# Dropping two doubly computed blocks of group 0, and regrouping the idle products of the opening

## The chip, the cores and the metric

The kernel runs on one core of a Trainium2 chip. The metric is the device time of one execution in microseconds. The core has a matrix engine (TensorE, PE in the profile, whose weight loads are listed apart as PEld), a vector engine (VectorE, DVE), a scalar engine (ScalarE, ACT), a general engine (GpSimd, POOL) and a synchronisation engine (SyncE, SP). Each runs its own instructions in order and waits for the others by semaphores. PSUM holds the results of TensorE in eight banks. Transfers between memory and the core are issued by POOL (the inputs) and SP (transposing loads and stores).

## What is computed

The reference is linear attention with a decay per head, followed by a two-layer perceptron with an exact GELU. Batch 4, heads 8, sequence 768, head size 64; the perceptron goes 512 to 2048 to 512.

```python
# attention, for each batch and head, blocks of 64 positions
intra = einsum('bhic,bhjc->bhij', qb, kb) * Dmask         # lam**(i-j) for i >= j
intra = einsum('bhij,bhjd->bhid', intra, vb)
inter = einsum('bhid,bhde->bhie', qb * lam_pow, kv_state)  # lam**(i+1)
out[:, :, sl] = intra + inter
kv_state = lam**64 * kv_state + einsum('bhsd,bhse->bhde', kb * rev_pow, vb)
# perceptron over all 4*768 = 3072 tokens
h = x @ w_in
g = 0.5 * h * (1 + erf(h / sqrt(2)))
result = g @ w_out
```

## The kernel before

The tokens are cut into chunks of 128 positions of one batch. A group is the same chunk position of all four batches: T = 512 tokens, and there are NG = 6 groups. Attention fills the activations `x_t` of a group (128 x 4 x 512, bf16), one quarter of the columns per batch (`empty`, line 337, a multiplication on VectorE). The perceptron `mlp(g)` (line 412) then works on the group.

The first product of a group has 16 blocks `kf` of 128 hidden units. A block is four TensorE products of 128x128 weights by 512 columns (`columns`, line 419), accumulated in one PSUM bank, then one GELU on ScalarE into `g_t` (line 430). The second product has 16 pieces p0 to p15 (line 455): four products each, with the weights `w_out_t`.

`mlp` returns a list of named blocks, and `run_blocks` (line 501) issues them in that order. A dictionary, written out by hand, gives the work to be issued ahead of a named block: loads, copies, and the attention of the next group (`visit`). Issue order is execution order on each engine.

With `n2 > 0`, a few blocks are split by columns, so that they can begin when only half of `x_t` is filled: a0 and a1 do columns 0 to 255 of blocks 0 and 1, and b0 and b1 the rest, with the GELU of all 512 columns behind each b. Group 0 is called as `mlp(0, 2)`, so n2 = 2 and n3 = 0. Line 482 then lists blocks m0 to m15 whole, from `n3`. Blocks 0 and 1 are in that list as well: they are computed by a0, a1, b0, b1 and again by m0 and m1, which write the same values to the same place. Their PSUM bank is chosen by line 427: blocks 0 and 1 use the banks `mo0` and `mo1` in both computations, the others alternate between two banks `mh`. Group 1 is called with n2 = 4 and n3 = 6, later groups with neither; in these no block is listed twice.

The opening, ahead of group 0's perceptron, is the attention of the first four chunks, which has no earlier state: transposes, `scores0`, masks, and `outputs0` (line 379), eight small products for each chunk which read the values `v_t` (one tile for chunks 0 and 1, one for 2 and 3). Into this the kernel puts idle products (`keep_warm`, line 494): 128x512 products of a zeroed tile into a bank that nobody reads. It issues one ahead of the four `outputs0`, and two behind each of them.

The inputs arrive in the order of the list on line 147, all issued by POOL: keys and queries of the first chunks, values `v_t`, then the first weights in five steps, `i0-2` (hidden blocks 0 and 1), `i2-4`, `i4-8`, `i8-12`, `i12-16`, each as two transfers; then the second weights in four steps `o0-4` to `o12-16`, mixed with the inputs of group 1. The semaphores of these transfers go round in eight, so transfer number i + 8 is issued only when number i has landed.

Of the kernel before, what the change touches and what calls it, by code (L numbers as in the profile page):

```python
# [15 lines left out]
def kernel(  # L16
# [19 lines left out]
    NK2 = d_ff // 128  # L36
    T = B * C
# [16 lines left out]
    def bank(shape, dtype, tag, name):  # L54
        return ps.tile(shape, dtype, tag=tag, name=name, bufs=BANKS[tag])
# [280 lines left out]
    def empty(c):  # L336
        nc.vector.tensor_mul(xT[c.g][:, :, c.b * C:(c.b + 1) * C], c.o, lam_o)  # L337
# [41 lines left out]
    def outputs0(n):  # L379
        c = live[n]  # L380
        c.o = bank([128, HP, C], F32, "at", "o_ps")
        issue([[(c.o[half(1 - hi), hp, :], c.v[:, 2 * hp + hi, :], c.sm[:, hp, hi, :], True) for hi in range(2)]
               for hp in range(HP)])
# [28 lines left out]
    def mlp(g, n2=0, n3=0):  # L412


        x_t = xT[g]
        g_t = g_pool.tile([128, NK2, T], BF16, tag="g", name="g_t")
        hs = {}

        def columns(kf, lo, up):
            for ki in range(NK1):  # L420
                nc.tensor.matmul(hs[kf][:, lo:up], w_in_t[:, ki, kf * 128:(kf + 1) * 128], x_t[:, ki, lo:up],  # L421
                                 start=(ki == 0 and lo == 0), stop=(ki == NK1 - 1), skip_group_check=True)

        def mm1(kf, lo, up, last):
            def run():
                if lo == 0:
                    hs[kf] = bank([128, T], F32, f"mo{kf}" if kf < min(n2, 2) else "mh", "h_ps")
                columns(kf, lo, up)
                if last:
                    nc.scalar.activation(g_t[:, kf, :up], hs[kf][:, :up], ACT.Gelu)  # L430
            return run

        def rest(kfs):
            def run():
                h_ps = bank([128, len(kfs), C], F32, "mh", "h_ps")
                for i, kf in enumerate(kfs):
                    for ki in range(NK1):
                        nc.tensor.matmul(h_ps[:, i, :], w_in_t[:, ki, kf * 128:(kf + 1) * 128], x_t[:, ki, T - C:],  # L438
                                         start=(i == 0 and ki == 0), stop=(ki == NK1 - 1), skip_group_check=True)
                nc.scalar.activation(g_t[:, kfs[0]:kfs[-1] + 1, T - C:], h_ps, ACT.Gelu)  # L440
            return run

        om = {}

        def store(io, ps_, w):
            n = w.stop - w.start
            o_sb = out_pool.tile([128, n], F32, tag=f"o_{n}", name="o_sb")
            r = io * S + g * C
            nc.scalar.copy(o_sb, ps_)  # L449
            if g == 0:  # L450
                held.append((r, w, o_sb))
            else:
                nc.sync.dma_start(out[r:r + C, w], o_sb)

        def mm2(io, part):
            def run():
                if part == 0:
                    om[io] = bank([128, d_model], F32, "mh" if g == 0 and io >= 2 else f"mo{io % 2}", "o2_ps")
                for kf in range(part * 4, part * 4 + 4):
                    nc.tensor.matmul(om[io], g_t[:, kf, io * C:(io + 1) * C], w_out_t[:, kf, :],  # L460
                                     start=(kf == 0), stop=(kf == NK2 - 1))
                if part == NK2 // 4 - 1:
                    store(io, om[io], slice(0, d_model))
            return run

        def mm2_half(io, h):
            def run():
                w = slice(h * (d_model // 2), (h + 1) * (d_model // 2))
                o2 = bank([128, d_model // 2], F32, f"mo{(io + h) % 2}", "o2_ps")
                for kf in range(NK2):  # L470
                    nc.tensor.matmul(o2, g_t[:, kf, io * C:(io + 1) * C], w_out_t[:, kf, w],  # L471
                                     start=(kf == 0), stop=(kf == NK2 - 1))
                store(io, o2, w)
            return run

        blocks = [(f"a{kf}", mm1(kf, 0, 2 * C, False)) for kf in range(n2)]

        blocks += [(f"b{kf}", mm1(kf, 2 * C, T - C if kf < n3 else T, True))
                   for kf in [*range(2, n2), *range(min(n2, 2))]]
        blocks += [(f"m{kf}", mm1(kf, 0, T - C, True)) for kf in range(n2, n3)]  # L480
        blocks += [(f"l{i}", rest(list(range(i, min(i + 4, n3))))) for i in range(0, n3, 4)]
        blocks += [(f"m{kf}", mm1(kf, 0, T, True)) for kf in range(n3, NK2)]
        if g == 0:
            second = [mm2(io, part) for part in range(4) for io in range(B)]
        elif g == NG - 1:
            second = [mm2(io, part) for io in range(B - 1) for part in range(4)]
            second += [mm2_half(B - 1, h) for h in range(2)]
        else:
            second = [mm2(io, part) for io in range(B) for part in range(4)]
        return blocks + [(f"p{i}", run) for i, run in enumerate(second)]  # L490
# [3 lines left out]
    def keep_warm(n):  # L494
        if not idle_ps:
            idle_ps[0] = bank([128, 512], F32, "mo0", "idle_ps")
        for _ in range(n):
            nc.tensor.matmul(idle_ps[0], idle[:, :128], idle, start=True, stop=True)  # L498
# [34 lines left out]
    scores0(3)  # L533
    make_lam()
    nc.scalar.activation(warm, pos, ACT.Gelu)
    keep_warm(1)
    for n in range(B):
        outputs0(n)
        empty(live[n])
        keep_warm(2)  # L540


    alloc_x(1)
# [11 lines left out]
    def ahead_of_group_1():  # L555
# [10 lines left out]
        begin(9)  # L566

    run_blocks(mlp(0, 2), {
        "m2": [ahead_of_group_1],
        "m6": [make_dmask] + [lambda n=n: decay_k0(n, nc.vector) for n in range(B)],  # L570
# [70 lines left out]
    for g in range(1, NG):  # L641
        if g + 1 < NG:
            alloc_x(g + 1)
        run_blocks(mlp(g, 4, 6) if g == 1 else mlp(g), plan_of(g))
# [29 lines left out]
```

## Time and profile before

| | us |
|---|---|
| median of the runs | 212.78 |
| the profiled execution, its own time | 212.92 |
| span of the profile (first to last instruction) | 211.1 |
| PE busy | 200.6 |
| POOL busy | 102.6 |
| ACT busy | 91.1 |
| DVE busy | 82.8 |

The span is 1.8 us shorter than the execution's time; what lies around it is outside the program's instructions. The profile's columns for a stretch of time (a timeline) are: start in us from the first instruction, length in us, engine, line, operation, what it writes and reads, shape, count, and in brackets the engine's idle time before it with what ended it. A row can stand for many instructions, and its length runs from the start of the first to the end of the last. The single record of a matmul includes its way through the array (0.38 us for a 128x512 product), while in a stream such products begin 0.22 us apart: a count of products is therefore turned into time by the distance of starts and not by the mean of the records. A few matmul records are missing: 62 are listed where 64 were issued.

### The profile page before, as it was taken

Reading aid. Unit: us, or ns where it says so; the run is one execution under the profiler, and the core shown is the slowest. Engines: PE = TensorE matmul, PEld = TensorE weight load, DVE = VectorE, ACT = ScalarE, POOL = GpSimd, SP = SyncE. Lnnn points to the kernel's source line nnn. Section 1 sums busy time; section 2 is a strip of 40 time slices with the busy share of each in tenths; the row PEclk is TensorE's granted clock in tenths of the full one; section 3 lists DMA queues with packets and bytes.
Section 4 is the critical chain, followed back from the end, with each engine's and each line's share of the span. In section 5 each row is a group of like instructions: output and inputs, shape, how many; then the busy total and the mean of one; then the engine's idle time right before and its main releaser. Section 6 shows DMA issues by size and latency. Waiting matters only on the chain.

```text
span 211.1 us, 5565 instructions
## 1 busy us (share of the span) xinstructions
PE 200.6 (95%) x2393; PEld 101.9 (48%) x2423; DVE 82.8 (39%) x185; ACT 91.1 (43%) x166; POOL 102.6 (49%) x144
## 2 busy tenths in 40 slices
PE   7789999999999999999999999999999999999992
PEld 2545445546754444444444444544444444444461
DVE  3578604037935556717525725532330331000000
ACT  5484664247666312266311456221556211665120
POOL 8978545798999008999169999300000000000000
PEclk9999999999999999999999999999999999999999
DMA  6999999999999995999999999412100021100121
GB/s 59 148 171 205 205 189 176 187 119 147 122 179 176 201 137 72 116 154 225 150 132 109 233 188 147 80 53 99 51 3 0 3 99 53 50 0 0 53 91 60
DMA packets 94713, 24.49 MB, mean 116 GB/s; under 512 B 86880, under 2 KB 91744, under 8 KB 94688
## 3 DMA queue, kind: packets, MB, share of 16 engines
q0 software_dynamic: 73536, 13.64, 79.6%
q1 hardware_dynamic: 21152, 10.50, 25.0%
q8 instruction: 19, 0.31, 0.6%
q14 instruction: 6, 0.05, 0.1%
HBM read 27.27 MB, written 6.29 MB: 159 GB/s over the span
## 4 chain that ended last, share of the span: by engine, by line
PE 86%; POOL 3%; DMA 3%; DVE 2%; ACT 2%; issue 2%; POOLq 0%
PE h_ps L421 38%; PE o_ps L460 37%; DMA v_t<-in_v_dram 3%; PE sc_ps L345 3%; POOL kq_t L82 3%; PE o_ps L345 2%; PE kv_ps L345 2%; PE o_ps L471 2%; ACT g_t L430 1%; PE idle_ps L498 1%; PE t_ps L250 1%; DVE x_t L337 1%; DVE sm L291 1%; PE h_ps L438 1%; PE t_ps L246 0%
## 5 line engine op out<-in xcount | busy, mean ns | idle before, releaser
L421 PE MATMUL h_ps<-x_t,w_in_t 128*128 128x512 bf16 (+3 forms) x404 | 85.8, 363 | 1.3 <-ACT g_t L430 0.2
L460 PE MATMUL o_ps<-w_out_t,g_t 128*128 128x512 bf16 x353 | 80.3, 379 | 1.9 <-issue 1.7
L430 ACT ACTIVATE g_t<-h_ps 128x512 bf16<-128x512 f32 (+1 forms) x98 | 57.3, 591 | 33.4 <-PE h_ps L421 33.4
L421 PEld LDWEIGHTS <-w_in_t 128*128 128x128 bf16 x416 | 39.3, 98 | 43.0 <-issue 1.4
L460 PEld LDWEIGHTS <-g_t 128*128 128x128 bf16 x368 | 34.6, 98 | 40.1
L337 DVE TENSOR_TENSOR x_t<-o_ps,lam_o 128x512 bf16<-128x512 f32 x24 | 16.6, 691 | 65.0 <-PE o_ps L345 64.8
L449 ACT COPY o_sb<-o_ps 128x512 f32<-128x512 f32 (+1 forms) x25 | 14.2, 568 | 63.9 <-PE o_ps L460 61.3
L280 POOL TENSOR_TENSOR vd<-vg_t,lam_v 128x512 bf16<-128x512 bf16 x20 | 21.3, 1070 | 19.7 <-DMA vg_t<-in_v_dram 18.7
L291 DVE TENSOR_TENSOR sm<-sc_ps,dmask 128x512 bf16<-128x512 f32 x20 | 13.6, 682 | 13.5 <-PE sc_ps L345 13.5
L71 POOL DMA_DIRECT2D k_t<-in_k_dram x20 | 18.1, 905 | 1.6 <-DMA w_out_t<-in_moe_w_out_dram 1.4
L106 POOL DMA_DIRECT2D vg_t<-in_v_dram x20 | 16.5, 847 | 2.1 <-DMA w_in_t<-in_moe_w_in_dram 2.0
L267 POOL COPY k<-k_t 64x256 bf16<-64x256 bf16 x34 | 13.7, 404 | 2.2 <-DMA k_t<-in_k_dram 1.2
L71 POOL DMA_DIRECT2D q_t<-in_q_dram x16 | 14.4, 901 | 0.0
L271 DVE COPY k<-k_t 64x256 bf16<-64x256 bf16 x34 | 11.8, 348 | 0.5
L345 PEld LDWEIGHTS <-kqT 64*64 64x64 bf16 (+1 forms) x352 | 7.4, 107 | 9.4 <-issue 8.3
L498 PE MATMUL idle_ps<-idle 128*128 128x512 bf16 x28 | 9.5, 441 | 1.3 <-DVE idle L151 1.2
L345 PE MATMUL sc_ps<-kqT 64*64 64x64 bf16 (+1 forms) x352 | 10.4, 197 | 0.1
L345 PE MATMUL o_ps<-sm,vg_t 64*64 64x64 bf16 x320 | 8.4, 193 | 0.0
L345 PE MATMUL kv_ps<-vd,k 64*64 64x64 bf16 x288 | 8.0, 193 | 0.0
L316 DVE TENSOR_TENSOR state<-t,lam_c 128x256 bf16<-128x256 f32 x16 | 7.0, 438 | 0.5
L125 POOL DMA_DIRECT2D w_in_t<-in_moe_w_in_dram x10 | 6.3, 688 | 1.4 <-DMA v_t<-in_v_dram 1.2
L345 PEld LDWEIGHTS <-vg_t 64*64 64x64 bf16 x320 | 6.8, 107 | 0.0
(73 smaller groups left out, 129.9 us busy)
## 6 DMA issues: line engine op xcount, KB each, us to landing
out_dram<-o_sb SPq DMA_DIRECT2D x23, 256.0 KB, 3.4
k_t<-in_k_dram POOLq DMA_DIRECT2D x20, 128.0 KB, 5.4
vg_t<-in_v_dram POOLq DMA_DIRECT2D x20, 128.0 KB, 8.2
w_out_t<-in_moe_w_out_dram POOLq DMA_DIRECT2D x4, 512.0 KB, 10.8
q_t<-in_q_dram POOLq DMA_DIRECT2D x16, 128.0 KB, 5.6
w_in_t<-in_moe_w_in_dram POOLq DMA_DIRECT2D x6, 256.0 KB, 7.2
kq_t<-in_k_dram POOLq DMA_DIRECT2D x4, 128.0 KB, 4.7
kq_t<-in_q_dram POOLq DMA_DIRECT2D x4, 128.0 KB, 4.1
```

The source lines that it names most:

```text
L71: nc.gpsimd.dma_start(t, dram[name][b, :, g * C:(g + 1) * C, :].rearrange("h si d -> si h d"))
L106: nc.gpsimd.dma_start(t[half(hi), u], src[hi, s:s + L])
L267: same.tensor_copy(c.k2[half(hi), hi], k_r[half(hi), :, hi, :])
L271: copy(c.k2[half(hi), 1 - hi], k_r[half(1 - hi), :, hi, :])
L280: nc.gpsimd.tensor_mul(vd[n], of_group(n), lam_vb)
L291: nc.vector.tensor_mul(c.sm, c.sc, dmask)
L337: nc.vector.tensor_mul(xT[c.g][:, :, c.b * C:(c.b + 1) * C], c.o, lam_o)
L345: nc.tensor.matmul(out_, lhsT, rhs, start=start, stop=True, skip_group_check=True)
L421: nc.tensor.matmul(hs[kf][:, lo:up], w_in_t[:, ki, kf * 128:(kf + 1) * 128], x_t[:, ki, lo:up], start=(ki == 0 and lo == 0), stop=(ki == N ...
L430: nc.scalar.activation(g_t[:, kf, :up], hs[kf][:, :up], ACT.Gelu)
L449: nc.scalar.copy(o_sb, ps_)
L460: nc.tensor.matmul(om[io], g_t[:, kf, io * C:(io + 1) * C], w_out_t[:, kf, :], start=(kf == 0), stop=(kf == NK2 - 1))
```

## The change

Three edits. Line 482 starts the list of whole blocks behind those that were computed by halves, so m0 and m1 fall away: eight 128x512 products on TensorE and two GELUs on ScalarE. Of the idle products, two instead of one go ahead of the four `outputs0`; and behind them there are none after the first and third and one after the second and fourth, in place of two after each. No other instruction is added, removed or reordered on any engine.

```diff
-        blocks += [(f"m{kf}", mm1(kf, 0, T, True)) for kf in range(n3, NK2)]
+        blocks += [(f"m{kf}", mm1(kf, 0, T, True)) for kf in range(max(n2, n3), NK2)]
...
     nc.scalar.activation(warm, pos, ACT.Gelu)
-    keep_warm(1)
+    keep_warm(2)
     for n in range(B):
         outputs0(n)
         empty(live[n])
-        keep_warm(2)
+        if n % 2:
+            keep_warm(1)
```

## The prediction

> **What bounds the kernel now.** I read the page's busy times first, then the chain that ended last, then the timeline of TensorE around the two edits, then that of GpSimd, which issues the loads.
>
> ```profile
> PE 200.6 (95%) x2393; PEld 101.9 (48%) x2423; DVE 82.8 (39%) x185; ACT 91.1 (43%) x166; POOL 102.6 (49%) x144
> ...
> DMA  6999999999999995999999999412100021100121
> ```
>
> TensorE is busy for 95% of the span, so work taken from it can count. But the transfer engines are full too, from slice 2 to slice 25, slice 16 apart (5 to 132 us): how far TensorE can be moved ahead is decided by when loads land. The edits lie at 13 to 22 us. TensorE's timeline there, with its first row and the end of group 0's first product:
>
> ```profile
> 1.19 3.25 PE L498 MATMUL idle_ps<-idle 128*128 128x512 bf16 x8 [1.19 <-DVE idle L151]
> ...
> 14.39 0.41 PE L345 MATMUL o_ps<-sm,v_t 128*64 128x128 bf16 x8 [0.71 <-DMA v_t<-in_v_dram]
> 14.74 0.61 PE L498 MATMUL idle_ps<-idle 128*128 128x512 bf16 x2
> 15.28 0.41 PE L345 MATMUL o_ps<-sm,v_t 128*64 128x128 bf16 x8
> ...
> 17.39 0.61 PE L498 MATMUL idle_ps<-idle 128*128 128x512 bf16 x2
> 18.05 1.91 PE L421 MATMUL h_ps<-x_t,w_in_t 128*128 128x256 bf16 x16
> 20.20 13.97 PE L421 MATMUL h_ps<-x_t,w_in_t 128*128 128x512 bf16 x62 [0.25 <-ACT g_t L430]
> 34.11 0.69 PE L345 MATMUL kv_ps<-v_t,kd 128*64 128x64 bf16 x32
> ```
>
> The outputs of the opening begin at 14.39, when `v_t` lands. From there to 34.11 TensorE waits once, 0.25 us at 20.20: m0 waits for the GELU of b0, whose bank it takes again. The chain that ended last runs through all these rows, the idle products too, so here time saved is time gained until something else is late.
>
> **The sum, step by step.** I follow block m4, the first from which both kernels have the same work left.
>
> Before: sixteen blocks from 20.20 to 34.11 are 13.91 / 16 = 0.869 us each (0.217 a product). m4 began at 20.20 + 4 x 0.869 = 23.68.
>
> 1. *Idle products.* The second one ahead of the outputs falls into the 0.71 us that TensorE waits for `v_t` and needs 0.22: nothing, so long as that wait is over 0.22. Were the cover gone, it would cost 0.22. Behind 14.39 an `outputs0` takes 0.35 (14.39 to 14.74), and the rows from 14.74 to 15.28 give 0.54 for two idle products, so 0.31 for one (0.54 less the 0.22 by which two follow each other, rounded). The new order is out, out, idle, out, out, idle: 4 x 0.35 + 2 x 0.31 = 2.02, and about 0.1 more for the last idle product to leave the bank that a0 takes. a0 could start at 16.5, and not at 18.05. The second `v_t` tile is no hindrance: its packets end at 15.0, and the third output comes at 15.4.
>
> 2. *`x_t`.* Vector engine: its last mask ended at 15.01; four `empty` in a row, 0.60 apart and 0.69 long, then end at 15.6, 16.2, 16.9 and 17.5. a0 needs the first two, b0 (0.87 behind a0) all four. Neither is late by this.
>
> 3. *The first weights, a wait that was hidden.* The loads as GpSimd issued them, and behind them the view of the tile `w_in_t` for the one issue at 14.54:
>
> ```profile
> 10.15 3.19 POOL L125 DMA_DIRECT2D w_in_t<-in_moe_w_in_dram  x5
> 14.54 0.62 POOL L125 DMA_DIRECT2D w_in_t<-in_moe_w_in_dram  x1 [1.20 <-DMA v_t<-in_v_dram]
> ...
> 20.85 0.76 POOL L128 DMA_DIRECT2D w_out_t<-in_moe_w_out_dram  x1 [0.51 <-DMA w_in_t<-in_moe_w_in_dram]
> ```
>
> ```profile
> L125 POOL DMA_DIRECT2D w_in_t<-in_moe_w_in_dram x1: 617/617/617, 14.5 to 14.5; - x1
> ...
> DMA to landing us min/median/max: 6.0/6.0/6.0
> ```
>
> `i0-2` was issued at 10.15 and 10.76; in the same view of its two issues landing takes 5.9, so the second half is there at 16.66. `v_t` needed 0.13 from landing (14.26) to the first product, so a0 starts at 16.79, not 16.5. Its sixteen half-width products begin 0.109 apart (1.74, from the row at 18.05): m2 starts at 18.53. `i2-4` (issued by 12.0, landing in 5.9) is there at 17.9. m2 and m3 take 1.74: m4 could start at 20.27. Of its weights `i4-8`, the second half was issued only at 14.54, when a transfer of `v_t` eight earlier had landed, and it landed 6.0 later, at 20.57; the row at 20.85 is a load that waited for that same landing. So m4 starts at 20.57 + 0.13 = **20.70**, and waits 0.43.
>
> 4. *m0 and m1.* 8 x 0.217 = 1.74 of products and the wait at 20.20 go (0.41 from the start that m0 could have had, 18.05 + 1.74 = 19.79). m2 takes an `mh` bank, long free. Their two GELUs (0.6 each) leave ScalarE, which was waiting for TensorE at each block: nothing on the path.
>
> Sum: m4 comes 23.68 - 20.70 = **2.98 us earlier**. Counting TensorE's work alone would give 1.55 + 0.41 + 1.74 = 3.70; the loads take 0.72 of it back.
>
> **Does it reach the end?** What is not driven by TensorE must be ready 3 us earlier than it was used. With margins in the trace before: `i8-12` landed by 23.1, used at 27.2; `o0-4` landed at 28.2, used at 34.7; `o8-12` at 39.0, used at 43.3; chunk 5's keys at 40.0, used at 44.8; the transposed queries of chunk 8 at 59.3, used at 64.0. The two closest are GpSimd's products of late values:
>
> ```profile
> 37.19 2.04 POOL L280 TENSOR_TENSOR vd<-vg_t,lam_v 128x512 bf16<-128x512 bf16 x2 [1.01 <-DMA vg_t<-in_v_dram]
> ...
> 79.78 1.04 POOL L280 TENSOR_TENSOR vd<-vg_t,lam_v 128x512 bf16<-128x512 bf16 x1 [10.83 <-DMA vg_t<-in_v_dram]
> 80.78 0.85 POOL L267 COPY k<-k_t 64x256 bf16<-64x256 bf16 x2
> ```
>
> The first of the pair at 37.19 ends at 38.23 and was used by the states of chunk 4 at 41.85: 3.62, of which 0.6 is left. The copy at 80.78 ends at 81.62 and was used by those of chunk 12 at 85.36: 3.74, of which 0.8 is left. From chunk 13 on margins exceed 5 us. None of these loads waits for TensorE; one store that does (issued by SP at 75.68, behind the GELUs and copies of group 1) can move up at most to 74.4 and share the transfer engines 1.2 us longer with the values of group 3. That is at most 1.2 us later for chunk 12, so 0 to 0.4 on the path; I take nothing.
>
> So 212.92 - 2.98 = 209.94 by the profiled execution, which stands 0.14 over the median: **209.9 us**, 1.4% less. A difference of 2% is about what a measurement of this kernel can tell from no change.
>
> **The pace of TensorE.** The first row above has eight idle products in 3.25 us, 0.41 each; from 4.7 on they come at 0.22. So TensorE can run at half pace, and idle products might be what prevents it. In the new opening its waits are 0.3 (before a0) and 0.43 (before m4); the kernel before has 0.71 and keeps its pace. The Trainium skill, "TensorE: Matmul & The Clock Gate", Part 1, says that the clock halves after an idle window of about 3.4 us and opens after a busy one; and its Part 4 that transposes do not count as busy in the same way, which speaks against taking idle products from an opening made of transposes. By the idle window the sum stands; no wait here is near it, and no run here shows a closing.
>
> **Rivals.**
>
> *All of TensorE's saving* (0.15): the loads of the opening are quicker than in the profiled execution, by 0.7 relative to `v_t`. Then 3.70: 209.1 us. For: the edge is only tenths of a microsecond. Against: the transfer engines are full there.
>
> *A late value* (0.12): a load that loses more than 0.6 to 0.8 us stops the states of chunk 4 or 12; or the first weights come later. It takes back 0.3 to 1.0: 210.2 to 210.9.
>
> *One spell of half pace* (0.05): as long as the 3.25 us at the start, with 8 products where 15 would go, a loss of 1.5. m4 is at 20.27 + 1.5 = 21.8, 1.1 later than by its load: 211.0.
>
> *Slower, by the pace* (0.03): the half pace starts at a0 and lasts. a0 to b1 take 3.26 and m2 and m3 3.25, so m4 starts at 23.3, and each further block loses 0.76. If it holds beyond m4 (some 8 us) the gain is gone; through m7, 0.4 gained and 3.0 lost, 215.5. For: five idle products go. Against: it would need a spell over twice that at the start, with TensorE almost always busy.
>
> That the change does not do what it says has no chance: the instruction lists of both kernels differ by thirteen products and two GELUs and no order.
>
> **Numbers.** Forecast 0.65, for 209.5 to 210.3 (0.43 either way, the wait at m4 doubled or gone). The range takes in all of TensorE's saving and the late value: 208.9 to 211.0. Faster by over 2% (below 208.5) needs more than the 3.70 that were taken away: 0.03. Slower by over 2% (above 217.0): 0.02. Within: 0.95.
>
> **What would show it.** In the changed profile: the outputs in two pairs from about 14.4, a0 near 16.8 released by `w_in_t` and not by an idle product; a wait of about 0.4 before m4, released by `w_in_t`; no wait for a GELU ahead of m2; the states after group 0's first product at 31.1, and every later row of TensorE 3.0 earlier to the end. A product row at 0.4 each behind 14 us would show the half pace; a wait at chunk 4's or 12's states the late value. The prediction is wrong if the opening's loads land at other distances from `v_t` than here.

## The result, and the profile after

The kernel after takes **210.75 us** (median), the kernel before, run beside it, 212.85: a ratio of 0.9902, 95% interval 0.9877 to 0.9926, so 0.7 to 1.2% less. Forecast were 209.9 us, 1.4% less, and no more than 2%; the median lies above the narrow range (209.5 to 210.3) and inside the wide one (208.9 to 211.0). The profiled execution took 210.59 us with a span of 208.8; before it was 212.92 and 211.1. So 2.3 us of the forecast 2.98 are there, by the medians 2.1. In some executions of most kernels here the time is 2 to 9 us longer; the ratios leave these out, the medians count them, and the one of them that was profiled, that of the first experiment below, ran its opening at half pace.

The busy times and the occupation of the transfer engines, from the page:

```profile
span 208.8 us, 5565 instructions
...
PE 201.0 (96%) x2410; PEld 100.8 (48%) x2410; DVE 84.0 (40%) x185; ACT 89.9 (43%) x164; POOL 102.6 (49%) x144
...
DMA  5999999999999996999996999944100021100121
```

TensorE is no less busy, though thirteen products of 0.22 are gone: it has 2410 of its records and not 2393. Of the kernel before, 30 records of products are missing (it has 2423 weight loads, one for each product), so the busy time can't be compared to tenths. ScalarE lost its two GELUs (164 for 166). The places are read from TensorE's timeline, from the last idle products ahead of the outputs to the block m4 and the states behind the first product:

```profile
13.48 0.61 PE L498 MATMUL idle_ps<-idle 128*128 128x512 bf16 x2
14.67 0.64 PE L345 MATMUL o_ps<-sm,v_t 128*64 128x128 bf16 x16 [0.58 <-DMA v_t<-in_v_dram]
15.24 0.39 PE L498 MATMUL idle_ps<-idle 128*128 128x512 bf16 x1
15.98 0.64 PE L345 MATMUL o_ps<-sm,v_t 128*64 128x128 bf16 x16 [0.35 <-DVE x_t L337]
16.55 0.39 PE L498 MATMUL idle_ps<-idle 128*128 128x512 bf16 x1
17.02 3.63 PE L421 MATMUL h_ps<-x_t,w_in_t 128*128 128x256 bf16 x24
20.99 10.52 PE L421 MATMUL h_ps<-x_t,w_in_t 128*128 128x512 bf16 x48 [0.34 <-DMA w_in_t<-in_moe_w_in_dram]
31.44 0.69 PE L345 MATMUL kv_ps<-v_t,kd 128*64 128x64 bf16 x32
```

The two pairs are there, b1 is followed by m2 without a wait, and m4 waits for its weights. From the first output (14.67) to the states (31.44) it is 16.77 us; before it was 14.39 to 34.11, 19.72. That is 2.95 less, against a forecast of 2.98. So the loss is elsewhere. A table of distances between the same instructions in the two timelines finds it:

| stretch | before | after | difference |
|---|---|---|---|
| start to the first output (landing of `v_t`) | 14.39 | 14.67 | +0.28 |
| to the states behind group 0's first product | 19.72 | 16.77 | -2.95 |
| to the scores of chunk 7 | 20.64 | 20.48 | -0.16 |
| to the scores of chunk 8 | 9.24 | 9.69 | +0.45 |
| to the scores of chunk 13 | 29.61 | 29.67 | +0.06 |
| to the end | 117.49 | 117.48 | -0.01 |

The first row is the scatter of a landing. The 0.45 lies where the perceptron turns from group 0 to group 1. The chain that ended last runs through VectorE there:

```profile
14.82 6.04 DMA w_in_t<-in_moe_w_in_dram
20.86 0.14 issue
...
51.87 0.44 DVE t L314
52.33 0.93 DVE state L316
53.26 0.60 DVE x_t L337
```

The start of this fence is m4's wait: a transfer that takes 6.04 us from issue to landing, as in the kernel before. Its end shows a row that the prediction never looked at: `state L316`, the product that makes the state for chunk 10, takes 0.93 us. VectorE's timeline of after, then of before, for the same three instructions:

```profile
51.87 0.42 DVE L314 TENSOR_TENSOR t<-kv_ps,t 128x256 f32<-128x256 f32 x1
52.33 0.93 DVE L316 TENSOR_TENSOR state<-t,lam_c 128x256 bf16<-128x256 f32 x1
53.18 0.68 DVE L337 TENSOR_TENSOR x_t<-o_ps,lam_o 128x512 bf16<-128x512 f32 x1
```

```profile
54.69 0.42 DVE L314 TENSOR_TENSOR t<-kv_ps,t 128x256 f32<-128x256 f32 x1
55.15 0.42 DVE L316 TENSOR_TENSOR state<-t,lam_c 128x256 bf16<-128x256 f32 x1
55.55 0.69 DVE L337 TENSOR_TENSOR x_t<-o_ps,lam_o 128x512 bf16<-128x512 f32 x1
```

One operation took 0.51 more; the neighbours, which read PSUM, took the same. What ran on GpSimd meanwhile, with the issue of the second half of `i4-8` above it:

```profile
14.82 0.61 POOL L125 DMA_DIRECT2D w_in_t<-in_moe_w_in_dram  x1 [0.35 <-DMA v_t<-in_v_dram]
...
51.94 1.04 POOL L280 TENSOR_TENSOR vd<-vg_t,lam_v 128x512 bf16<-128x512 bf16 x1 [1.39 <-DMA vg_t<-in_v_dram]
52.93 1.04 POOL L267 COPY k<-k_t 64x256 bf16<-64x256 bf16 x2
```

In the kernel before the first of these two rows was:

```profile
50.42 1.09 POOL L280 TENSOR_TENSOR vd<-vg_t,lam_v 128x512 bf16<-128x512 bf16 x1 [0.56 <-DMA vg_t<-in_v_dram]
```

GpSimd waits for `vg_t`, a load, and does not move ahead with TensorE: its product came 1.5 us later than before (where it ran beside a copy of VectorE that took 0.95), while VectorE came 2.8 us earlier and met it with the state. The state ended at 53.26, 0.28 behind the end of GpSimd's product (52.98). The Trainium skill, "SBUF — State Buffer", section "SBUF: two separate sides", says that VectorE and GpSimd share one pair of ports, which one of them holds for a whole instruction while the other stands still, and that a VectorE operation with two inputs in SBUF takes part in it. VectorE's three rows agree: only the product of `t` and `lam_c`, both in SBUF, grew. So do all the profiles of this case: 41 of their 224 state products took longer than alone (0.49 to 1.31 us) beside a product or copy of GpSimd that was under way when they began, and every one of the 41 ended 0.27 to 0.29 us behind that instruction.

TensorE's waits of after:

```profile
PE o_ps L345 <- DMA v_t<-in_v_dram: 0.6, 1, 0.6
PE o_ps L345 <- DVE x_t L337: 0.4, 1, 0.4
PE h_ps L421 <- DMA w_in_t<-in_moe_w_in_dram: 0.3, 1, 0.3
PE h_ps L421 <- DVE x_t L337: 0.3, 1, 0.3
```

The third is m4's. The fourth, at 53.91, stands behind the late state: the `x_t` that VectorE makes next. It is 0.29 of the 0.45; behind it the chain goes on over VectorE and ScalarE, whose copy of `mid` and five GELUs follow.

### The profile page after: what moved, and what is told of

Same layout as the page of the kernel before. It is cut to its first block, busy times and chain, and to the rows that moved or that the text cites. A ratio compares the mean times of both kernels' runs of the same rounds, so it can differ in the third digit from the quotient of the medians.

```text
span 208.8 us, 5565 instructions
## 1 busy us (share of the span) xinstructions
PE 201.0 (96%) x2410; PEld 100.8 (48%) x2410; DVE 84.0 (40%) x185; ACT 89.9 (43%) x164; POOL 102.6 (49%) x144
## 4 chain that ended last, share of the span: by engine, by line
PE 84%; DMA 6%; POOL 3%; DVE 2%; ACT 2%; issue 1%; POOLq 0%
PE o_ps L460 38%; PE h_ps L421 36%; DMA v_t<-in_v_dram 3%; PE sc_ps L345 3%; DMA w_in_t<-in_moe_w_in_dram 3%; POOL kq_t L82 3%; PE kv_ps L345 2%; PE o_ps L471 2%; PE o_ps L345 2%; ACT g_t L430 1%; PE t_ps L250 1%; DVE x_t L337 1%; DVE sm L291 1%; PE h_ps L438 1%; DVE state L316 0%
## 5 line engine op out<-in xcount | busy, mean ns | idle before, releaser
L421 PE MATMUL h_ps<-x_t,w_in_t 128*128 128x512 bf16 (+3 forms) x408 | 84.8, 363 | 1.0 <-DMA w_in_t<-in_moe_w_in_dram 0.3
L460 PE MATMUL o_ps<-w_out_t,g_t 128*128 128x512 bf16 x368 | 83.2, 379 | 0.0
L430 ACT ACTIVATE g_t<-h_ps 128x512 bf16<-128x512 f32 (+1 forms) x96 | 56.1, 591 | 32.1 <-PE h_ps L421 32.1
L421 PEld LDWEIGHTS <-w_in_t 128*128 128x128 bf16 x408 | 38.4, 98 | 42.5 <-issue 2.2
L316 DVE TENSOR_TENSOR state<-t,lam_c 128x256 bf16<-128x256 f32 x16 | 8.4, 527 | 0.6
```

## The experiments

The first four split the change and try its forecast waits; the next ask what holds the pace; the rest move what met on VectorE and GpSimd. Distances as in the table above are used throughout, since the first output comes at 14.02 to 14.77 us from run to run, in some held by `v_t` and in some by TensorE's own work ahead of it. Diffs of the first two are against the kernel before, those of the others against the kernel after.

### The blocks alone

```diff
-        blocks += [(f"m{kf}", mm1(kf, 0, T, True)) for kf in range(n3, NK2)]
+        blocks += [(f"m{kf}", mm1(kf, 0, T, True)) for kf in range(max(n2, n3), NK2)]
```

> Only m0 and m1 go; the idle products stay as before. Theory (the opening is TensorE's until the load of the weights of m4 lands, 6.3 us behind the values): a0 stays 3.8 us behind the landing of the values, m2 follows b1 without a wait, and m4 starts 7.25 us behind that landing, in place of 9.4 before; its weights are there by then, no wait. So 2.15 us earlier at m4. In the first steps of group 1 a product of VectorE may again run into GpSimd and give up to 0.45 back: 210.7 to 211.2 us. Rival (each removed piece gives its own work, 1.74 us of products and the wait for a GELU, and nothing binds): also 2.15, but then the idle products alone must give the rest of what the whole change gives, which is 0 by it.

Median 212.12 us, ratio 0.9952 (0.9923 to 0.998); the runs in the ratio go from 210.74 to 212.95. The profile, whose opening ran at half pace, still gives the stretch behind a0, where the pace was full again. TensorE's timeline of this kernel:

```profile
23.36 13.99 PE L421 MATMUL h_ps<-x_t,w_in_t 128*128 128x256 bf16 x70
37.28 0.69 PE L345 MATMUL kv_ps<-v_t,kd 128*64 128x64 bf16 x32
```

One unbroken row: 13.92 from a0 to the states, where before took 16.06 (18.05 to 34.11). The 2.14 are step 4's 1.74 of products and 0.41 of wait; a0 is late by the kept idle products, and in this profile by the half pace too, and m4 does not wait. The lowest run agrees with that; by the ratio only 1.0 us arrives, and no profile here shows where the rest goes. That stays open.

### The idle products alone

```diff
-    keep_warm(1)
+    keep_warm(2)
     for n in range(B):
         outputs0(n)
         empty(live[n])
-        keep_warm(2)
+        if n % 2:
+            keep_warm(1)
```

> Only the idle products change; m0 and m1 are computed again. Theory: a0 starts 2.5 us behind the landing of the values (third and fourth outputs still wait for their values), the rest up to m4 takes as long as before, wait for the GELU ahead of m0 included; m4 starts 8.1 us behind the landing, 1.3 us earlier than before: 211.5 us, up to 0.45 more if VectorE meets GpSimd in group 1. With the first run the two parts sum to 3.45 us, of which the whole change has only 2.1, since both draw on the same limit, the load of the weights of m4. Rival (idle products held the pace, or their time was hidden): no gain, 212.6 to 213.1.

Median 212.44, ratio 0.9991 (0.9963 to 1.0019), its runs from 211.51 to 213.94. The profiled execution, 211.65, is among the lowest; in it the way from the first output to the states is 18.49, which is 1.23 less than before. The wait for the GELU that m0 has is kept, as TensorE's timeline shows:

```profile
19.09 5.12 PE L421 MATMUL h_ps<-x_t,w_in_t 128*128 128x512 bf16 x22 [0.25 <-ACT g_t L430]
```

So 1.23 here and 2.14 above would make 3.37 if they simply added; together they make 2.95, because m4 then comes to its weights and waits. By the ratios the parts make 0.2 and 1.0 us, less than the 2.1 of the whole; that scatter behind the opening eats a part of the gain in each is not shown.

### The wait at m4 taken away

In group 0, blocks 4 to 7 read the weights of blocks 0 to 3, which have landed; the time of the loads and of everything else stays.

```diff
+            kw = kf - 4 if g == 0 and 4 <= kf < 8 else kf
             for ki in range(NK1):
-                nc.tensor.matmul(hs[kf][:, lo:up], w_in_t[:, ki, kf * 128:(kf + 1) * 128], ...
+                nc.tensor.matmul(hs[kf][:, lo:up], w_in_t[:, ki, kw * 128:(kw + 1) * 128], ...
```

> The changed kernel, but blocks m4 to m7 of group 0 multiply with the weights of blocks 0 to 3, so that part of the result is not the reference's: it takes away the wait for the weights of m4 and leaves all loads as they are. Theory: m4 starts right behind m3, 0.4 to 0.5 us earlier than in the changed kernel, m8 does not wait, and the end comes 0.3 to 0.5 us earlier if nothing later takes it: 210.2 to 210.5 us against 210.7. Rival (the loss is behind group 0 and this wait is covered there): the same time as the changed kernel.

Median 210.32 (four runs), ratio 0.9889 (0.9841 to 0.9937). TensorE's timeline:

```profile
16.99 7.30 PE L422 MATMUL h_ps<-x_t,w_in_t 128*128 128x256 bf16 x40
```

The row runs through m4 without a break, and from a0 to the states it takes 13.92 in place of 14.42: the wait at m4 is worth 0.50 (forecast 0.43), and it is what stands between this opening and TensorE's own work. The profile shows that; the intervals of the two ratios (0.9889 and 0.9902) overlap.

### The late values of group 1 issued later

To let VectorE pass first, GpSimd's product for chunk 8 is moved from a0 to b2, behind the loads issued there.

```diff
-                "a0": [lambda: values(n), lambda: request(n + 1), lambda: store_held(slice(0, 2))],
+                "a0": [lambda: request(n + 1), lambda: store_held(slice(0, 2))],
...
-                "b2": [lambda: fetch(n + 2, n + 3)],
+                "b2": [lambda: fetch(n + 2, n + 3), lambda: values(n)],
```

> The changed kernel, but GpSimd computes the decayed values and the copy of chunk 8 behind the issue of the loads of chunks 10 and 11, some 2 us later. Theory (in the changed kernel GpSimd's product held up the product that makes the state of chunk 10 on VectorE, 0.93 us in place of 0.42, on the chain): that row takes 0.42, the scores of chunk 8 come 0.45 us earlier relative to the states behind group 0's first product, and the time is 0.3 to 0.5 us less than the changed kernel's: 210.2 to 210.5. Rival (the 0.45 us were lost to loads or to the order on TensorE): the distance from those states to the scores of chunk 8 stays at 30.1 us and the time at 210.7.

Median 211.6, ratio 0.9928 (0.9885 to 0.9972). It failed. The loads of chunks 10 and 11 are now issued from 50.71 on and not from 53.91, and the same state product took longer still. VectorE's row, then GpSimd's rows from that time:

```profile
52.24 1.19 DVE L316 TENSOR_TENSOR state<-t,lam_c 128x256 bf16<-128x256 f32 x1
```

```profile
52.45 0.96 POOL L71 DMA_DIRECT2D k_t<-in_k_dram  x1
53.31 0.97 POOL L71 DMA_DIRECT2D q_t<-in_q_dram  x1
54.20 1.15 POOL L280 TENSOR_TENSOR vd<-vg_t,lam_v 128x512 bf16<-128x512 bf16 x1
```

No product or copy of GpSimd ran beside it, only issues of loads. Beside such issues the state product kept its 0.42 in every other case, as in the kernel before at 55.15; why it did not here stays open.

The waits of TensorE behind the opening:

```profile
PE kv_ps L345 <- issue: 1.2, 1, 1.2
PE sc_ps L345 <- DMA kqT<-q_t: 0.9, 1, 0.9
PE h_ps L421 <- DVE x_t L337: 0.6, 1, 0.6
```

The second is the transposed queries of chunk 8, there at 62.76 and not at 59.53 though asked for at the same time (54.03 and 54.08): by this one pair of profiles, a load issued 3 us earlier is paid by another. The third stands behind the longer state product. The first is a wait that no semaphore explains; more of these below.

### The kernel after, looked at again

The same kernel, for the scatter of one profile.

> The changed kernel once more, for a second profile. Theory (the advance is cut by what TensorE does not drive, and that varies from one execution to the next): the opening again stands by the landing of the values (a0 2.3 to 2.9 us behind the first output, a wait ahead of m4 that ends with the landing of its weights), and the time is explained by m4's start plus the excess of the state product of VectorE in group 1 over 0.42 us plus any wait for late values; 210.2 without such waits, up to 211.9 with them. Rival (a fixed loss): the same rows at the same places as in the first profile, 210.6 +- 0.2.

210.84 us. The opening is the same (16.81 from first output to states). The state product of chunk 10 took 0.53 this time, yet the stretch from chunk 7 to 8 took 9.96, since TensorE stood still before two small products (its timeline):

```profile
55.49 0.22 PE L345 MATMUL o_ps<-kqT,state 64*64 64x64 bf16 x2 [0.76 <-issue]
```

So two costs vary from one execution to the next: the length of the collision, and a wait that the profile files under "issue".

### No idle products behind the first eight

```diff
-    keep_warm(1)
...
-    keep_warm(2)
     for n in range(B):
         outputs0(n)
         empty(live[n])
-        if n % 2:
-            keep_warm(1)
```

(and likewise each `keep_warm` between the first eight and these).

> The changed kernel with no idle product at all behind the first eight. Theory (what bounds the opening is loads; the pace is held by the small products and transposes too): the outputs begin when the values land, a0 at the landing of its weights, m4 as in the changed kernel: 210.2 to 210.9 us. Rival (idle products hold the pace of TensorE, since transposes do not): products of the opening and of the first blocks come at 0.4 us each for 3 us or more, and the time is 1.5 us or more above the changed kernel's: 212.3 to 217.

Median 212.7, ratio 1.0 (0.9978 to 1.0021); the lowest run, 212.15, is above the median of after by 1.4. TensorE's timeline, then that of ScalarE:

```profile
14.02 1.07 PE L345 MATMUL o_ps<-sm,v_t 128*64 128x128 bf16 x16
16.06 1.07 PE L345 MATMUL o_ps<-sm,v_t 128*64 128x128 bf16 x16 [0.97 <-DVE x_t L337]
17.10 7.13 PE L421 MATMUL h_ps<-x_t,w_in_t 128*128 128x256 bf16 x32
```

```profile
19.86 1.34 ACT L430 ACTIVATE g_t<-h_ps 128x512 bf16<-128x512 f32 x2 [2.65 <-PE h_ps L421]
```

Sixteen output products take 1.07 and not 0.64, the sixteen half-width products from a0 take 3.51 and not 1.75, so that ScalarE waits 2.65 for b0 (1.66 in after); from 20.6 on products come at 0.216 again. The rival of the half pace is a real one: here the half pace of the start holds for 19 us, not for one spell of 3.25. From the first output to the states it takes 18.56 for 16.77, so 1.8 us are lost. Yet TensorE never stood still for over 1 us between 1.19 and 20.6. The Trainium skill, "TensorE: Matmul & The Clock Gate", Part 1, has the clock rise after a busy window and fall after an idle one of about 3.4 us; by that alone it should have risen. Part 4 of that page, that transposes do not count as busy in the same way, agrees with this run: the work in the opening is transposes and small products. The granted clock of the profile reads 1.00 all through that time, so the pace must be read from the rows. Idle products do not make the full pace certain: in the profile of the blocks alone, with as many of them among the transposes as in after, it was the half pace too until about 20.5 us (two idle products took 1.03 at 19.60).

### The state of chunk 10 made later

The product on VectorE that met GpSimd is issued at m5, where VectorE has time; chunk 10 needs it some 20 us later.

```diff
+    later = []
...
-        nc.vector.tensor_mul(new, t2, lam_cb)
+        later.append(lambda: nc.vector.tensor_mul(new, t2, lam_cb))
+        if c.n != 6:
+            later.pop()()
...
-                "m5": [lambda: keys(n), lambda: request(n + 2, n + 3), lambda: store_held(slice(2, B))],
+                "m5": [lambda: keys(n), lambda: later.pop()(), lambda: request(n + 2, n + 3), lambda: store_held(slice(2, B))],
```

> The changed kernel, but VectorE makes the state of chunk 10 some 3 us later (ahead of m5 of group 1), off the chain; GpSimd and all loads stay as they are. Theory (that product, held up by GpSimd, delayed what VectorE, ScalarE and TensorE do behind it): the filling of the next quarter of x_t moves up 0.6 us to the end of its outputs, the wait of TensorE at the third quarter (0.29 us) goes, the distance from the states behind group 0's first product to the scores of chunk 8 is 29.5 to 29.7 us in place of 30.2, and the time is 0.4 to 0.6 less than the changed kernel's (210.0 to 210.3 against 210.7). Rival (VectorE had slack there): distance and time stay.

Median 211.08 (four runs), ratio 0.9909 (0.9873 to 0.9945). From chunk 7 to chunk 8 it is 9.36, and less a wait of 0.20 under "issue" 9.16, no more than the 9.24 of before. But TensorE has other waits, first in its list, then in GpSimd's timeline:

```profile
PE o_ps L348 <- issue: 1.0, 2, 0.8
...
PE kv_ps L348 <- POOL k L268: 0.5, 1, 0.5
```

```profile
82.65 1.04 POOL L281 TENSOR_TENSOR vd<-vg_t,lam_v 128x512 bf16<-128x512 bf16 x1 [10.71 <-DMA vg_t<-in_v_dram]
83.64 0.85 POOL L268 COPY k<-k_t 64x256 bf16<-64x256 bf16 x2
```

This is the late value of chunk 12 that the prediction had as a rival, with the price it gave (0.3 to 1.0): GpSimd's product ends its copy at 84.48, where the kernel before had it at 81.62, and the states of chunk 12 wait 0.47.

### The same, with `i4-8` cut in two

```diff
-    ask("k0 q0 k1 q1 k2 q2 k3 q3 v0 v2 i0-2 i2-4 i4-8 i8-12 i12-16 "
+    ask("k0 q0 k1 q1 k2 q2 k3 q3 v0 v2 i0-2 i2-4 i4-6 i6-8 i8-12 i12-16 "
```

> As the one before, and the load of the weights of blocks 4 to 7 is split in two steps, those of 4 and 5 first. Theory: what m4 waits for lands 1.3 us earlier, its wait (0.3 us of idle time, 0.5 from its possible start) goes, and nothing is late at m6: both gains add, 0.9 to 1.1 us under the changed kernel: 209.6 to 209.9. Rival (smaller transfers land later, or the gain is taken by late values in group 1): no faster than the one before.

Median 213.06, ratio 0.9975 (0.9941 to 1.0009). The wait at m4 is gone (13.92 from a0 to the states), but two more transfers stand ahead of all later ones, and in the ring of eight each now waits for the landing of another. The last part of group 1's values, issued at 26.43 as in after (26.49), landed at 38.99 and not at 37.54; from TensorE's waits:

```profile
PE kv_ps L348 <- POOL vd L281: 1.3, 1, 1.3
```

The values of chunk 4, for which the prediction left a margin of 0.6, come 1.3 too late. So neither of the two gains reached the end.

### The kernel after, timed again

> The changed kernel once more, beside the two that follow. Theory (its advance at m4 is steady, what it loses behind group 0 varies): the same as in the first comparison, 210.7 us by the median of its runs, single runs from 210.2 (nothing lost behind group 0) to 211.9; in its profile m4 starts 6.3 to 6.6 us behind the landing of the values. Rival (a fixed loss): all runs within 0.3 us.

Median 211.25, ratio 0.9917 (0.9891 to 0.9942), beside the next two. Its profile (210.96) has the state product at 0.77 with 9.52 from chunk 7 to 8, and a wait of 0.72 under "issue" at 131.23.

### The state made later, timed again

The edit is that of the state alone.

> The kernel with the state product of chunk 10 made later, timed with more runs than before. Theory: 0.3 to 0.5 us under the changed kernel of the same call, 210.2 to 210.5; the distance from the scores of chunk 7 to those of chunk 8 is 9.2 to 9.4 us where no product waits in between (9.7 in the changed kernel). Rival (the collision moves to another row or another wait takes its place): the same time as the changed kernel.

Median 211.23, ratio 0.9905 (0.9873 to 0.9937): no different from after. VectorE's timeline shows the product gone from its place, TensorE's what was there instead, and the chain what came later:

```profile
51.90 0.42 DVE L315 TENSOR_TENSOR t<-kv_ps,t 128x256 f32<-128x256 f32 x1
52.76 0.69 DVE L340 TENSOR_TENSOR x_t<-o_ps,lam_o 128x512 bf16<-128x512 f32 x1 [0.43 <-PE o_ps L348]
```

```profile
55.24 0.22 PE L348 MATMUL o_ps<-kqT,state 64*64 64x64 bf16 x2 [0.47 <-issue]
```

```profile
81.65 1.01 POOL vd L281
82.66 0.35 POOL k L268
...
83.06 0.41 POOL k L268
```

VectorE now waits for TensorE (0.43) and no longer the other way. Less the 0.47 the stretch is 9.17. In this profile what was won there is given back: chunk 12's copies, ending at 83.47, are on the chain.

### The state later, and three blocks of weights with the first

Cut otherwise, the list keeps its count of transfers: m4's weights come with those of m2 and m3.

```diff
-    ask("k0 q0 k1 q1 k2 q2 k3 q3 v0 v2 i0-2 i2-4 i4-8 i8-12 i12-16 "
+    ask("k0 q0 k1 q1 k2 q2 k3 q3 v0 v2 i0-2 i2-5 i5-8 i8-12 i12-16 "
```

> As the one before, and the loads of the first weights are cut at block 5 in place of block 4 (steps 2 to 5 and 5 to 8, as many transfers and as many bytes as before). Theory: m2 waits 0.2 to 0.3 us for the larger step, m3 and m4 follow without a wait, and m5 finds its weights; m5 starts 0.2 to 0.4 us earlier relative to the landing of the values, nothing behind moves, as no transfer is added: 209.9 to 210.3. Rival (the order of landing decides, not the cut): m2 waits as long as m4 did, and the time is that of the one before.

Median 211.53, ratio 0.9916 (0.989 to 0.9942). From a0 to the states it takes 14.14, the 0.28 less that were expected, and from chunk 7 to 8 it takes 9.24; the time is the same within the intervals. In its profile from chunk 8 to 13 it is 30.20, where before had 29.61.

### All that, and two stores later

The stores that SP issued at m5 (the prediction named them, at 75.68 before, as sharing the transfer engines with chunk 12's values) go behind the loads issued at p6.

```diff
-                "m5": [lambda: keys(n), lambda: later.pop()(), lambda: request(n + 2, n + 3), lambda: store_held(slice(2, B))],
+                "m5": [lambda: keys(n), lambda: later.pop()(), lambda: request(n + 2, n + 3)],
...
-                "p6": [lambda: keys(n + 3), lambda: fetch(n + 6, n + 7), lambda: request(n + 6, n + 7)],
+                "p6": [lambda: keys(n + 3), lambda: fetch(n + 6, n + 7), lambda: request(n + 6, n + 7),
+                       lambda: store_held(slice(2, B))],
```

> As the one before (state product later, loads cut at block 5), and two of the four held stores of group 0 (256 KB each) go out behind the transposes of chunks 14 and 15, some 20 us later. Theory (the values of chunk 12 come late because the transfer engines are full until they land, and TensorE now reaches their use within a microsecond): GpSimd begins them 0.5 to 2 us earlier, by 80.5 us in place of 81.1 to 82.6, the states of chunk 12 never wait, and the runs lie closer together: 209.9 to 210.5 us by the median. Rival (the values are late for another reason, or the scatter comes from elsewhere): they begin when they did, and the median is that of the kernel before it, 210.9.

Median 210.52, ratio 0.9874 (0.9841 to 0.9906). GpSimd's timeline:

```profile
79.15 1.04 POOL L281 TENSOR_TENSOR vd<-vg_t,lam_v 128x512 bf16<-128x512 bf16 x1 [8.00 <-DVE x_t L340]
80.14 0.97 POOL L268 COPY k<-k_t 64x256 bf16<-64x256 bf16 x2
```

Chunk 12's copies end at 81.11, where the other kernels with the change's shorter opening have them at 82.3 to 84.9; nothing waits for them. This is the lowest ratio found for a kernel that computes everything, from six runs; from the kernel after it can't be told apart by them, since the intervals overlap. Its own profile has a wait of 0.73 for `v_t` and one of 0.53 under "issue".

## Why the prediction was right

Right were the direction and the mechanism of the opening: the loads take back a part of TensorE's saving. The size at the end was not: 210.75 lies above the 209.5 to 210.3 that were given 0.65. It lies in the band of the late value (210.2 to 210.9, given 0.12), but what took the time was something else, so that band fits by luck.

- *What bounds the kernel.* Of the 2.95 taken from TensorE ahead of 34 us, 2.61 arrived at the end by the distances (2.33 by the span, in which `v_t` landed 0.28 later); from chunk 8 on both kernels go alike to 0.06. Of the 0.65 by which the span falls short of the forecast 2.98, the landing makes 0.28 and the stretch to chunk 8 0.45; the stretch ahead of it gives 0.16 back.
- *Step 1, idle products.* a0 came 2.35 behind the first output, forecast 2.40 (16.79 less 14.39), but by another road. "The second `v_t` tile is no hindrance" failed: the third output came at 15.98 and not at 15.4. The second tile's transfer landed at 15.85, whatever its packets did by 15.0. The record names the `x_t` of chunk 0, done at 15.88, and by it alone the two can't be told apart; in two other profiles (no wait at m4, and stores later) the same wait, 0.83 and 0.73, is filed under `v_t`. It cost nothing only because `i0-2` landed at 16.93, as the last idle product left a0's bank (16.94); in the profiles of the state later and of the three blocks of weights a0's wait is filed under `w_in_t` (0.34 and 0.28), as forecast.
- *Step 2, `x_t`.* Right in the opening. Where it is filled for group 1 nobody looked; that is the 0.45.
- *Step 3, first weights.* The wait is right, and its size too: 0.49 (m3 ended its turn at 20.50) against 0.43, and taking it away gave 0.50. The reason given for the landing does not hold, that the second half of `i4-8` was issued late, behind a landing of `v_t`: in the ten profiles that tell its landing it was issued at 13.48 to 14.82 and landed at 20.50 to 20.89 all the same. So the landing does not follow the issue, and that it came 6.3 behind `v_t` in both kernels (up to 7.7 in the others) is luck.
- *Step 4, m0 and m1.* Right: 2.14 for the blocks alone, against 1.74 + 0.41.
- *Does it reach the end?* Here the term is mis-sized: for what lies behind group 0 nothing was taken, and in the profile 0.45 belongs there. The margins were worked out for loads and for GpSimd's products that TensorE waits for; what was left out is that GpSimd, tied to loads, does not move with VectorE (1.5 us later against 2.8 us earlier), so that the two meet on new instructions. Eight profiles order it, waits under "issue" taken off: where the state product takes 0.42 (before, and the idle products alone) the stretch is 9.24 and 9.25; at 0.53 (after, looked at again) 9.20; at 0.60 (the blocks alone), 0.67 (no idle products) and 0.69 (no wait at m4) 9.48, 9.43 and 9.45; at 0.77 (the second timing) 9.52, at 0.93 (after) 9.69. With the product moved away it is 9.16 to 9.24 in all five profiles (0.20 to 0.53 taken off in four). So the stall is there from 0.60 on, is largest where the product takes longest, and is gone with the product. The kernel with the values issued later, 1.19 and 10.96 with other waits, is left out of this list.
- *The rivals.* The late value of chunk 12 is a neighbour and not far: after has it at 82.34, in time by 0.7 us, and the kernel with the state later stood 0.5 for it. The half pace did not come, but its price was wrong: without the idle products it lasted 19 us and cost 1.8, between the two rivals (1.1 for one spell of 3.25 us, 5.6 for a lasting one).

By its two ratios this kernel gains 2.1 and 1.8 us; its lowest runs (210.2) gain 0.5 to 0.8 more and lie 0.3 above the forecast. The profiles show waits of that size: the collision (0.1 to 0.8), chunk 12, and waits under "issue" (0.2 to 1.2). How often each comes was not measured.

## What to carry to other kernels

When work is taken from one engine, the others do not all move with it: an engine tied to loads goes by the loads. So look not only for who is late by the shift, but for which instructions newly overlap, and whether they share a port. A margin of a few tenths against a transfer in full engines is a chance and not a margin; and idle products that seem to do nothing may help to hold the pace, so take them away a few at a time and read the pace from the rows.

## What the runs showed of the hardware

A VectorE product with both inputs in SBUF (the 128x256 state product) took 0.42 to 0.43 us alone. Begun while a product or copy of GpSimd was under way, it ended 0.27 to 0.29 us behind that instruction and so took up to 1.31; the VectorE sums that read PSUM took 0.40 to 0.43 in both cases. One state product took 1.19 beside issues of loads alone, and is not explained.

A half pace of TensorE, once there, held through an opening of transposes and small products without an idle time over 1 us, and ended at 20.6 us, 3.5 us into the dense products. In another profile it held with idle products among the transposes, TensorE being busy 12.6 of the 14 us from 5 to 19, and ended at about 20.5, ahead of the dense products.

TensorE stood still for 0.4 to 1.2 us with nothing in the profile to release it in eight of the fourteen profiles, and often at the same place of its program: chunk 7's outputs, at 55.49, 56.19, 55.24 and 55.14 in four of them. A weight load stands before each product, and the records of the loads are complete; twice the number of loads ahead of such a place lies 176 or 178 behind a multiple of 256 at all eleven such waits. The Trainium skill, "Runtime: NRT & Kernel Launch", section "Instruction fetch mechanics", says that instructions are fetched in blocks of 256 by transfers of their own and that this is mostly hidden. The page of after lists such a queue (19 packets of instructions, 0.31 MB, so 16 KB each; TensorE has 4842 records, or 18.9 times 256). A block that comes late through full transfer engines would explain the place and the scatter. But at each of these waits the last packet of that queue had ended 1.2 to 3.3 us before TensorE went on, and no run here tried it: this stays an argument.
